# Second tile of q by the casting queue, a new order of the beginning, and whole feed-forward blocks in the first token group

## The chip, the cores and the metric

The kernel runs on one core of a Trainium2 chip. The metric is the device time of one execution in microseconds, as the median of several runs. A profile of one execution gives its span and the work of each engine: PE (matrix products, with PEld for its weight loads), DVE (vector engine), ACT (scalar engine), POOL (GpSimd), and SP, which only issues transfers here.

## The reference

Two steps follow each other. The first is a cosine-weighted linear attention over 8 batches of 8 heads, 576 positions and 64 dimensions. The second is a gated feed-forward block on 4608 tokens of 512 values, with 1536 hidden values.

```
phi(x) = concat(relu(x) * cos(theta), relu(x) * sin(theta))     theta = pi/2 * position / 576
kv  = sum over s of phi(k)[s, f] * v[s, d]        z = sum over s of phi(k)[s, f]
out = (phi(q) @ kv) / (phi(q) @ z + 1e-6)
x   = out, heads side by side: 4608 tokens x 512
g   = x @ w_gate      val = x @ w_val
y   = (silu(g) * val) @ w_out
```

All inputs and the output are float32 in memory. The kernel computes in bfloat16 and accumulates in float32.

## The kernel before, in words

**Tokens.** Each batch has NC = 9 slots of 64 positions. Two slots make a tile of 128 tokens, and four tiles make a group of 512 tokens (GH = 8 slots, T = 512). There are nine groups. The first group is tiles 0 to 3 and needs slots 0 to 7 of batch 0. Its beginning is written by hand; the groups after it follow a plan of slots (`at`, `slot`).

**Loads.** The sync queue (`nc.sync`, SP) carries what must come first, in float32: v of batch 0 in two parts, q slots 0 and 1, k of batch 0 in three parts, then q slots 2 and 3 (`load_first`, L115 to L126). The casting queue (`nc.gpsimd`, POOL) carries the rest and turns float32 into bfloat16 on its way: q slots 4 to 7 of batch 0, the gate and value weights in pieces (`load_w`), k, v and q of batch 1, the output weights (`load_wo`), then batch 2. One small copy on POOL (`hold`, L574) keeps it from issuing before the first part of v is there. `CUT` says where a batch's q is split into two loads.

**The beginning.** A list of words (L619) gives the order in which the instructions of the first group are written. Each engine has its own queue and works through it in that order, waiting where it must. The words, with the tile or part in their digits and the engine after @:

- `cq` casts a slot of q from float32 to bfloat16 (`cast_q`, L337); `tq` turns a tile of q on PE by products with the identity (`turn_q`, L341); `qr` is the relu of the turned q (`relu_turned`); `qw` multiplies it by cosines (part 0) or sines (part 1) on DVE (`weight_q`, L359).
- `rk` is the relu of a part of k, from float32 to bfloat16 (L223); `kv` the products of k and v (`kv_first`, L304); `kvo` the copy of a half of kv from the accumulation banks to memory (`kv_first_out`, L326). `kvo00` and `kvo01` are the two halves for j = 0, `kvo10` and `kvo11` those for j = 1.
- `a` is the attention product of a tile (`a_tile`, L366), `den` and `rec` the denominators and their reciprocals, `x` the normalised tile, `xt` its turning on PE, `xc` the copy of the turned tile to `xT`.
- `G`, `V`, `s`, `m` are one feed-forward block of 128 hidden values: gate products, value products, silu on ACT, multiplication on DVE. `G2.01` is block 2 for tiles 0 and 1, `G1.0` block 1 for tile 0 alone.
- `z` are products with zeros that nobody reads; they keep PE running.

In `turn_q` the tiles 0 and 1 come from `qf`, which `cq` has written, with four full transposes. The tiles 2 and 3 come from the bfloat16 tile `raws[0, "q"]`, in eight transposes of half width.

**The accumulation banks.** There are 8 banks of 512 float32 columns. `take` hands out those used longest ago. A block for 256 tokens fits gate and value into one bank; for 512 tokens it takes two.

**The later blocks of the first group.** Blocks 6 to 11 run in two halves of 256 tokens: blocks f and f+1 for the first half ("a"), then both for the second ("b"). After each, `slot` runs what is planned there: the relu of k of batch 1 (a8, a9), `vmul` for batch 1 (a10, a11, b8, b9), the turning of the last slot of q of batch 0 (b9), and at b11 the turning of q of batch 1 and its kv products. Then come 12 pieces of output products (`steps0`, L707) with tiles 4 to 7 of attention between them (`a_` at slots (0, 0) to (1, 3)). From then on groups run whole blocks of 512 tokens.

Of the kernel before, what the change touches and what calls it, by code (L numbers as in the profile page):

```python
# [10 lines left out]
FP32 = mybir.dt.float32  # L11
# [7 lines left out]
def kernel(  # L19
# [11 lines left out]
    B, H, S, D = q.shape  # L31
    P = 128
    G = H // 2
    J = G // 2
    SH = 64
    NC = S // SH
    d_model, d_ff = moe_w_gate.shape
    KC = d_model // P
    FC = d_ff // P
# [3 lines left out]
    GH = 8  # L43
# [3 lines left out]
    consts = ctx.enter_context(tc.tile_pool(name="consts", bufs=1))  # L47
# [18 lines left out]
    def take(n, hold=None):  # L66

        free = [b for b in range(0, 8, n) if not any(b <= x < b + n for r in held.values() for x in r)]
        b0 = min(free, key=lambda b: sorted(used[b:b + n], reverse=True))
        if hold is not None:  # L70
            held[hold] = range(b0, b0 + n)
        touch(range(b0, b0 + n))
        return banks[:, b0] if n == 1 else banks[:, b0:b0 + n]
# [6 lines left out]
    def give_back(hold):  # L80
        touch(held.pop(hold))
# [4 lines left out]
    def source(b, nm):  # L86
        t = {"q": q, "k": k, "v": v}[nm]
        return t[b].rearrange("(g e) (p c) d -> (e p) g (c d)", e=2, c=NC)

    def raw_of(b, nm):  # L90
        if (b, nm) not in raws:
            raws[b, nm] = raw.tile([P, G, NC, D], BF16, name=f"raw_{nm}")
        return raws[b, nm]

    def load(b, nm, parts=1):
        t, sv, n = raw_of(b, nm), source(b, nm), G // parts
        for i in range(parts):
            sl = slice(i * n, (i + 1) * n)
            nc.gpsimd.dma_start(out=t[:, sl].rearrange("p g c d -> p g (c d)"), in_=sv[:, sl])

    def load_slots(b, nm, lo, hi):
        nc.gpsimd.dma_start(out=raw_of(b, nm)[:, :, lo:hi].rearrange("p g c d -> p g (c d)"),
                            in_=source(b, nm)[:, :, lo * D:hi * D])


    CUT = (4, 7)
    wo_sb = consts.tile([P, FC, d_model], BF16)
    hts = [consts.tile([P, FC, T], BF16, name=f"ht_{i}") for i in range(2)]
    first = {"q": consts.tile([P, G, CUT[0], D], FP32, name="first_q")}

    for nm, home in (("v", wo_sb), ("k", hts[1])):
        flat = home.rearrange("p a b -> p (a b)")[:, 0:2 * G * NC * D]
# [2 lines left out]
    def load_first(nm, gs, lo=0, hi=NC):  # L115
        nc.sync.dma_start(out=first[nm][:, gs, lo:hi].rearrange("p g c d -> p g (c d)"),  # L116
                          in_=source(0, nm)[:, gs, lo * D:hi * D])
# [5 lines left out]
    load_first("k", slice(0, 2))  # L123
    load_first("k", slice(2, 4), 0, KCUT)
    load_first("k", slice(2, 4), KCUT, NC)
    load_first("q", slice(0, G), 2, 4)  # L126
    NW = 8
    pos = consts.tile([P, NC], FP32)
    nc.gpsimd.iota(pos, pattern=[[1, NC]], base=0, channel_multiplier=NC, allow_small_or_imprecise_dtypes=True)
# [6 lines left out]
    for j in range(2):  # L136
        t = consts.tile([P, 8 * J * D1], BF16, name=f"kvd_{j}")
# [50 lines left out]
    for j in range(2):  # L188
        t = consts.tile([P, G, NC, 2, W], BF16, name=f"v2_{j}")
# [10 lines left out]
    def load_w(i, n=2):  # L200

        fs = slice(i * P, (i + n) * P)
        nc.gpsimd.dma_start(out=wg_sb[:, :, fs], in_=wg_r[:, :, fs])
        nc.gpsimd.dma_start(out=wv_sb[:, :, fs], in_=wv_r[:, :, fs])

    def load_wo(i):
        cs = slice(4 * i, 4 * i + 4)
        nc.gpsimd.dma_start(out=wo_sb[:, cs], in_=wo_r[:, cs])
# [10 lines left out]
    def relu_k(b, lo, hi, eng):  # L219
        o = raw_of(b, "k")[:, lo:hi]  # L220
        relu_op(eng, o, o)
# [38 lines left out]
    def qturn_pe(b, j, lo, hi, eng):  # L260
        ps = take(1).bitcast(BF16).rearrange("p (c x) -> p c x", x=P)
        for c in range(lo, hi):
            for i in range(2):
                nc.tensor.transpose(out=ps[i * D:(i + 1) * D, c - lo], in_=raws[b, "q"][:, 2 * j + i, c],  # L264
                                    identity=ident)
        relu_op(eng, qt_of(b)[:, :, j, lo:hi].rearrange("p e c s -> p c e s"),
                ps[:, 0:hi - lo].rearrange("p c (e s) -> p c e s", e=2))
# [33 lines left out]
    def kv_free(b):  # L301
        give_back(("kv", b))
# [38 lines left out]
    def turn_q(t):  # L341
        ps = take(1, ("tq", t)).bitcast(BF16).rearrange("p (y e s) -> p y e s", e=2, s=SH)
        for j in range(J):
            for c in range(2):
                y = 2 * j + c
                if t < 2:
                    nc.tensor.transpose(out=ps[:, y].rearrange("p e s -> p (e s)"),
                                        in_=qf[:, c, j].rearrange("p i d -> p (i d)"), identity=ident)
                    continue
                for i in range(2):  # L350
                    nc.tensor.transpose(out=ps[i * D:(i + 1) * D, y].rearrange("p e s -> p (e s)"),  # L351
                                        in_=raws[0, "q"][:, 2 * j + i, 2 * t + c], identity=ident)
        st["tq", t] = ps[:, 0:2 * J].rearrange("p y e s -> p e y s")
# [136 lines left out]
    def ffn_mm(tg, fc, lo=0, hi=GH, which=(0, 1)):  # L490

        n = (hi - lo) * SH
        ts = slice(lo // 2, hi // 2)
        fs = slice(fc * P, (fc + 1) * P)
        if 0 in which:
            if 2 * n <= 512:
                both = take(1, ("f", tg, fc, lo))
                st["f", tg, fc, lo] = [both[:, 0:n], both[:, n:2 * n]]
            else:
                st["f", tg, fc, lo] = [take(1)[:, 0:n] for _ in range(2)]  # L500
        for i in which:
            for kc in range(KC):
                nc.tensor.matmul(out=st["f", tg, fc, lo][i], lhsT=(wg_sb, wv_sb)[i][:, kc, fs], rhs=xT[tg][:, ts, kc],  # L503
                                 start=(kc == 0), stop=(kc == KC - 1))
# [14 lines left out]
    def ffn_act(*a):  # L519
        ffn_silu(*a)  # L520
        ffn_mul(*a)

    def ffn_fc(*a):

        ffn_mm(*a)
        ffn_act(*a)
# [45 lines left out]
    hold = consts.tile([P, 1], FP32)  # L572
    hold2 = consts.tile([1, 2], BF16)
    nc.gpsimd.tensor_copy(out=hold, in_=first["v"][:, 1, 0, 0:1])  # L574
    load_slots(0, "q", CUT[0], NW)
    load_w(0, 1)
    load_w(1, 1)
    for i in (2, 4, 6):
# [3 lines left out]
    load_slots(0, "q", NW, NC)  # L582
    load_w(10)
    load(1, "v", 2)
    load_slots(1, "q", 0, CUT[1])
    load_wo(0)
    load_wo(1)
    load_wo(2)
    load_slots(1, "q", CUT[1], NC)
    for nm in ("q", "k", "v"):  # L590
        load(2, nm)

# [4 lines left out]
    def at(s, *fns):  # L597
        plan.setdefault(s, []).extend(fns)

    def slot(s):  # L600
        for f in plan.pop(s, ()):
            f()

    def a_(t, j):
        return lambda: (a_half(t, j), x_norm(t) if j else None)
# [2 lines left out]
        return lambda: x_turn(t, fast)  # L608

    def q_(b, j, part, eng="act"):  # L610
        lo, hi = ((0, CUT[b]), (CUT[b], NC))[part]
        return lambda: qturn_pe(b, j, lo, hi, eng)


# [2 lines left out]


    words = """  # L619
        cq0@act cq1@act tq0 qr0@dve rk1.0@act rk0.0@dve qw0.0 qw0.1 z6 kv0.0 rk2.0@act rk3.0@dve rk2.1@act  # L620
        kv1.0 kvo01@dve rk3.1@act cq3@dve kv1.1 cq2@dve kvo00@dve tq1 kvo10@act a0.0 qr1@dve kvo11@act qw1.1
        z2 a0.1 qw1.0 tq2 den0 rec0 a1.0 x0.0 qr2@act tq3 x0.1 xt0.0 a1.1 qw2.0 xc0.0@act xt0.1 qw2.1
        xc0.1@act den1 z2 a2.0 rec1 qr3@act G1.0 x1.0 a2.1 G0.0 s1.0 V0.0 qw3.0 s0.0 xt1.0 qw3.1 V1.0
        xc1.0@dve a3.0 a3.1 m0.0 G1.1 den3 G2.01 m1.0 s1.1 rec3 V1.1 x3.0 s2.01 G0.1 V0.1 s0.1 V2.01 m1.1
        m0.1 xt3.0 den2 m2.01 G3.01 rec2 V3.01 x2.0 s3.01 G4.01 xc3.0@dve G5.01 s4.01 m3.01 xt2.0 s5.01
        V4.01 xc2.0@dve V5.01 m4.01 G2.23 m5.01 G0.23 s2.23 V0.23 s0.23 G3.23 m0.23 V2.23 s3.23 G4.23 m2.23
        V4.23 s4.23 V3.23 m4.23 G1.23 m3.23 V1.23 s1.23 G5.23 m1.23 V5.23 s5.23 m5.23
    """.split()
    halves = (slice(0, KC // 2), slice(KC // 2, KC))
    for word in words:  # L630
        word, _, eng = word.partition("@")
        op, a, b = re.match(r"([A-Za-z]+)(\d+)\.?(\d*)", word).groups()
        whole, a, part = b not in ("0", "1") or a != "0", int(a), int(b or 0)
# [39 lines left out]
                ffn_mul(0, a, *span)  # L673


    order = []
    for f in range(6, FC, 2):
        order += [("a", g) for g in (f, f + 1)]
        order += [("b", g) for g in (f, f + 1)]

    def turn_last():
        for j in range(J):
            qturn_pe(0, j, NC - 1, NC, "act")
# [1 line left out]
    at("b9", turn_last)  # L685
    at("a8", lambda: relu_k(1, 0, 2, "dve"))
    at("a9", lambda: relu_k(1, 2, 4, "dve"))
    for g, s in enumerate(("a10", "a11", "b8", "b9")):
        at(s, lambda g=g: vmul(1, g))
    at("b11", q_(1, 0, 0), q_(1, 1, 0), lambda: kv_mm(1), lambda: kv_out(1))  # L690
    at((0, 0), lambda: kv_free(1), a_(4, 0))
    at((0, 1), a_(4, 1))
    at((0, 2), a_(5, 0))
    at((0, 3), a_(5, 1))
    at((1, 0), turn(4, True), a_(6, 0))
# [3 lines left out]
    at((2, 0), turn(6, True))  # L699
    at((2, 1), q_(1, 0, 1), q_(1, 1, 1))  # L700
    at((2, 2), turn(7, True))
    HALF = GH // 2
    for nm, f in order:
        ffn_fc(0, f, *((HALF, GH) if nm == "b" else (0, HALF)))
        slot(f"{nm}{f}")

    steps0 = [(piece, t) for piece in range(3) for t in range(2)] + [(piece, t) for t in (2, 3) for piece in range(3)]  # L707
    for i, (piece, t) in enumerate(steps0):
# [10 lines left out]
    for b in range(2, B):  # L719
        s0 = SLOTS * (b - 1)  # L720
# [16 lines left out]
    for t in range(2 * OUT, NTG * OUT):  # L737
        tg, i = divmod(t, OUT)
        s = SLOTS * (tg - 1) + (5 if tg > 2 else 4) + 2 * i
# [8 lines left out]
    for tg in range(1, NTG):  # L748
        s0 = SLOTS * tg
# [40 lines left out]
```

## Time and profile before

| What | Value |
|---|---|
| Time, median of 3 runs | 327.97 us (327.35 to 328.61) |
| Span of the profiled execution | 326.1 us (that run took 327.92 us) |
| Granted PE clock | 1.0 |
| First transfer issued by SP | 0.74 us |
| First transfer issued by POOL | 4.50 us |
| First feed-forward product | 18.07 us |
| First block for half of the tokens after the words (block 6) | 30.17 us |
| First output product | 43.16 us |
| First product of group 1 | 57.13 us |

Some landings, as start of issue plus the time to landing that the trace gives:

| Transfer | Queue | Issued | Landed |
|---|---|---|---|
| q slots 0, 1 | sync | 1.75 | 7.6 |
| k, heads of the first half | sync | 2.27 | 9.5 |
| k, second half, slots 0 to 4 | sync | 2.8 | 10.3 |
| k, second half, slots 5 to 8 | sync | 3.3 | 11.4 |
| q slots 2, 3 | sync | 3.84 | 13.65 |
| q slots 4 to 7 | casting | 4.50 | 13.0 |
| gate weights, block 0 | casting | 5.39 | 14.2 |
| value weights, block 1 | casting | 7.59 | 16.5 |
| gate / value weights, blocks 2 and 3 | casting | 8.32 / 9.05 | 17.7 / 19.1 |
| gate weights, blocks 4 and 5 | casting | 9.79 | 20.4 |
| gate / value weights, blocks 8 and 9 | casting | 16.81 / 18.01 | 28.6 / 30.5 |
| q of batch 1, slots 0 to 6 | casting | 27.51 | 38.3 |
| output weights, three parts | casting | 29.11, 31.04, 31.8 | 40.8, 43.3, 45.9 |

How to read the profile's lines. A line in order of time gives start and length in microseconds, engine, line of the code, operation, what it writes and reads, the number of instructions merged, and in brackets how long the engine stood idle before it and what released it. The chain of waits is followed back from the last instruction, at each step to what released it. A queue's line gives its packets, megabytes as written, and the time its packets took as a share of 16 engines.

### The profile page before, as it was taken

How to read it: one execution, taken by the hardware profiler on the slowest of the kernel's cores; microseconds unless marked ns; L12 is line 12 of the kernel's file. 1: busy time of each engine (PE TensorE's matmuls, PEld its weight loads, DVE VectorE, ACT ScalarE, POOL GpSimd, SP SyncE). 2: the span in 40 equal slices, each digit the busy share in tenths (PEclk: the TensorE clock that was granted, in tenths of full speed). 3: DMA queues.
4: the chain of work that ended last, by engine and by line, in shares of the span. 5: the costliest groups of instructions: out<-in, count | busy, mean ns of one | idle time of the engine just before them, and what ended most of it. 6: DMA issues, size and time to landing. Idle time of an engine off the chain costs nothing.

```text
span 326.1 us, 6192 instructions
## 1 busy us (share of the span) xinstructions
PE 318.7 (98%) x2459; PEld 165.0 (51%) x2470; DVE 182.3 (56%) x367; ACT 132.8 (41%) x248; POOL 34.1 (10%) x57
## 2 busy tenths in 40 slices
PE   8799999999999999999999999999999999999995
PEld 4488855454545444544454445444454445444443
DVE  7594857885575655575557555655664145423420
ACT  7353456843463336423543344343432133213311
POOL 6654300002001100020002000200000000000000
PEclk9999999999999999999999999999999999999999
DMA  7999999398867997799598949795921411140014
GB/s 259 224 199 197 207 204 211 62 132 137 162 117 95 163 140 146 110 157 158 121 124 127 181 110 136 108 184 116 138 51 34 99 32 32 36 105 21 2 32 97
DMA packets 71660, 40.51 MB, mean 124 GB/s; under 512 B 46672, under 2 KB 66384, under 8 KB 71632
## 3 DMA queue, kind: packets, MB, share of 16 engines
q1 hardware_dynamic: 49808, 22.55, 39.0%
q0 software_dynamic: 21664, 17.44, 35.2%
q8 instruction: 19, 0.31, 0.4%
q10 hardware_dynamic: 160, 0.13, 0.1%
q14 instruction: 9, 0.07, 0.1%
HBM read 37.75 MB, written 9.44 MB: 145 GB/s over the span
## 4 chain that ended last, share of the span: by engine, by line
PE 94%; DMA 3%; SPq 1%; issue 0%; ACT 0%; DVE 0%; ACTq 0%; DVEq 0%
PE banks L503 57%; PE banks L539 28%; DMA first_q<-in_q_dram 3%; PE banks L276 3%; PE banks L390 2%; SPq L116 1%; PE banks L475 1%; PE banks L434 1%; PE banks L372 1%; PE banks L558 1%; PE banks L264 0%; PE banks L149 0%; ACT ob L561 0%; PE banks L351 0%; DVE qf L339 0%
## 5 line engine op out<-in xcount | busy, mean ns | idle before, releaser
L514 DVE TENSOR_TENSOR ht<-sg,banks 128x512 bf16<-128x512 bf16 (+2 forms) x122 | 76.0, 625 | 67.2 <-PE banks L503 60.9
L509 ACT ACTIVATE sg<-banks 128x512 bf16<-128x512 f32 (+2 forms) x122 | 66.9, 548 | 113.8 <-PE banks L503 108.7
L503 PE MATMUL banks<-xT,wv_sb 128*128 128x512 bf16 (+2 forms) x488 | 112.8, 355 | 0.0
L503 PE MATMUL banks<-xT,wg_sb 128*128 128x512 bf16 (+2 forms) x488 | 112.8, 355 | 0.0
L539 PE MATMUL banks<-wo_sb,ht 128*128 128x512 bf16 x409 | 93.5, 379 | 0.6
L503 PEld LDWEIGHTS <-wv_sb 128*128 128x128 bf16 x488 | 47.1, 98 | 46.4
L503 PEld LDWEIGHTS <-wg_sb 128*128 128x128 bf16 x488 | 45.7, 98 | 41.5
L539 PEld LDWEIGHTS <-ht 128*128 128x128 bf16 x420 | 40.0, 98 | 45.2 <-issue 0.4
L546 ACT COPY ob<-banks 128x512 f32<-128x512 f32 x18 | 10.6, 586 | 51.4 <-PE banks L539 49.4
L232 DVE TENSOR_TENSOR r_q<-raw_q,tab 128x1152 bf16<-128x1152 bf16 x24 | 17.9, 753 | 20.2 <-ACT raw_q L215 20.2
L546 DVE COPY ob<-banks 128x512 f32<-128x512 f32 x17 | 11.7, 691 | 28.9 <-PE banks L539 28.0
L236 DVE TENSOR_TENSOR v<-raw_v,tab 128x1152 bf16<-128x1152 bf16 x31 | 23.0, 751 | 0.3 <-ACT raw_v L570 0.3
L411 DVE TENSOR_TENSOR x<-banks,rec 128x512 bf16<-128x512 f32 (+1 forms) x32 | 21.5, 674 | 1.1
L714 POOL COPY hold<-phit 1x2 bf16<-1x2 bf16 x5 | 0.9, 176 | 156.6 <-DMA phit<-r_q 156.6
L215 ACT ACTIVATE raw_k<-raw_k 128x576 bf16<-128x576 bf16 x24 | 16.0, 675 | 0.0
L215 ACT ACTIVATE raw_q<-raw_q 128x576 bf16<-128x576 bf16 x24 | 15.7, 680 | 0.5 <-DMA raw_q<-in_q_dram 0.5
L390 PEld LDWEIGHTS <-phit 128*128 128x128 bf16 (+1 forms) x240 | 9.9, 100 | 6.0 <-issue 1.3
L390 PE MATMUL banks<-kv,phit 128*128 128x65 bf16 (+1 forms) x240 | 11.5, 195 | 0.0
L149 PE MATMUL banks<-zeros 128*128 128x64 bf16 (+1 forms) x66 | 9.9, 310 | 1.0 <-DVE zeros L144 1.0
L299 DVE CAST kv<-banks 64x260 bf16<-64x260 f32 x12 | 5.1, 428 | 7.5 <-ACT kv L299 7.4
L276 PEld LDWEIGHTS <-raw_k 64*64 64x64 bf16 x504 | 7.5, 106 | 2.6 <-issue 2.1
L276 PE MATMUL banks<-v,raw_k 64*64 64x130 bf16 x504 | 8.7, 218 | 0.0
(80 smaller groups left out, 136.3 us busy)
## 6 DMA issues: line engine op xcount, KB each, us to landing
out_dram<-ob SPq DMA_DIRECT2D x70, 128.0 KB, 2.4
raw_k<-in_k_dram POOLq DMA_DIRECT2D x7, 576.0 KB, 9.7
raw_q<-in_q_dram POOLq DMA_DIRECT2D x6, 576.0 KB, 6.1
raw_v<-in_v_dram POOLq DMA_DIRECT2D x6, 576.0 KB, 12.3
wo_sb<-in_moe_w_out_dram POOLq DMA_DIRECT2D x3, 512.0 KB, 12.3
wg_sb<-in_moe_w_gate_dram POOLq DMA_DIRECT2D x5, 256.0 KB, 10.6
wv_sb<-in_moe_w_val_dram POOLq DMA_DIRECT2D x5, 256.0 KB, 10.0
wo_sb<-in_v_dram SPq DMA_DIRECT2D x2, 576.0 KB, 4.1
```

What stands on the lines that cost most here:

```text
L149: nc.tensor.matmul(out=ps, lhsT=zeros, rhs=zeros[:, 0:cols].unsqueeze(1).to_broadcast([P, 4, cols]), start=True, stop=True)
L215: nc.scalar.activation(out=out, in_=in_, func=AF.Relu)
L232: nc.vector.tensor_tensor(out=st[b, "q"][:, g], in0=o.unsqueeze(2).to_broadcast([P, NC, 2, D]), in1=tab, op=ALU.mult)
L236: nc.vector.tensor_tensor(out=v2s[b % 2][:, g, :, :, 0:D], in0=(first if b == 0 and g == 0 else {"v": raw_of(b, "v")})["v"][:, g].unsqueez ...
L276: nc.tensor.matmul(out=ps[i * D:(i + 1) * D, e, j * 2 * D1:(j + 1) * 2 * D1], lhsT=raws[b, "k"][es, g, c], rhs=v2s[b % 2][es, g, c, :, 0:D ...
L390: nc.tensor.matmul(out=ps[ms, e, g * D1:(g + 1) * D1], lhsT=phit[b][:, e, g, c:c + n].rearrange("p c s -> p (c s)"), rhs=kv2s[b % 2][:, e, ...
L411: nc.vector.tensor_tensor(out=st["x", t].rearrange("p (y e d) -> p e y d", e=2, d=D)[:, :, ys], in0=ps[:, :, 0:2 * J * D1].rearrange("p e ...
L503: nc.tensor.matmul(out=st["f", tg, fc, lo][i], lhsT=(wg_sb, wv_sb)[i][:, kc, fs], rhs=xT[tg][:, ts, kc], start=(kc == 0), stop=(kc == KC - 1))
L509: nc.scalar.activation(out=sg[:, 0:n], in_=st["f", tg, fc, lo][0], func=AF.Silu)
L514: nc.vector.tensor_tensor(out=hts[tg % 2][:, fc, r:r + n], in0=st.pop(("s", tg, fc, lo))[:, 0:n], in1=ps[1], op=ALU.mult)
L539: nc.tensor.matmul(out=o_ps[t], lhsT=hts[tg % 2][:, fc, r:r + P], rhs=wo_sb[:, fc], start=(fc == 0), stop=(fc == FC - 1))
L546: (nc.scalar.copy if t % 2 == 0 else nc.vector.tensor_copy)(out=ob, in_=ps)
```

## The change

The second tile of q (slots 2 and 3) leaves the sync queue. It goes as the first transfer into the casting queue, so it arrives as bfloat16 and needs no cast; its turning then uses the eight half-width transposes that tiles 2 and 3 use. The order of the beginning is written anew for this: copies of kv move to ACT, relus of k to DVE, tile 3 comes before tile 2, and the products of blocks 0, 4 and 5 are placed elsewhere. Blocks 6 to 11 of the first group run for all 512 tokens at once, so what was planned behind the halves gets new places: slot a of block f and slot b of block f now follow each other directly. The vmul of batch 1 moves to b9, a10, b10 and a11; tile 4's two attention halves stand side by side.

```diff
-    CUT = (4, 7)
+    QCUT = 2
+    CUT = 7
...
-    first = {"q": consts.tile([P, G, CUT[0], D], FP32, name="first_q")}
+    first = {"q": consts.tile([P, G, QCUT, D], FP32, name="first_q")}
...
-    load_first("q", slice(0, G), 2, 4)
...
-                if t < 2:
+                if t == 0:
...
-    load_slots(0, "q", CUT[0], NW)
+    load_slots(0, "q", QCUT, 4)
+    load_slots(0, "q", 4, NW)
...
-        cq0@act cq1@act tq0 qr0@dve rk1.0@act rk0.0@dve qw0.0 qw0.1 z6 kv0.0 rk2.0@act rk3.0@dve rk2.1@act
-        kv1.0 kvo01@dve rk3.1@act cq3@dve kv1.1 cq2@dve kvo00@dve tq1 kvo10@act a0.0 qr1@dve kvo11@act qw1.1
-        z2 a0.1 qw1.0 tq2 den0 rec0 a1.0 x0.0 qr2@act tq3 x0.1 xt0.0 a1.1 qw2.0 xc0.0@act xt0.1 qw2.1
-        xc0.1@act den1 z2 a2.0 rec1 qr3@act G1.0 x1.0 a2.1 G0.0 s1.0 V0.0 qw3.0 s0.0 xt1.0 qw3.1 V1.0
-        xc1.0@dve a3.0 a3.1 m0.0 G1.1 den3 G2.01 m1.0 s1.1 rec3 V1.1 x3.0 s2.01 G0.1 V0.1 s0.1 V2.01 m1.1
-        m0.1 xt3.0 den2 m2.01 G3.01 rec2 V3.01 x2.0 s3.01 G4.01 xc3.0@dve G5.01 s4.01 m3.01 xt2.0 s5.01
-        V4.01 xc2.0@dve V5.01 m4.01 G2.23 m5.01 G0.23 s2.23 V0.23 s0.23 G3.23 m0.23 V2.23 s3.23 G4.23 m2.23
-        V4.23 s4.23 V3.23 m4.23 G1.23 m3.23 V1.23 s1.23 G5.23 m1.23 V5.23 s5.23 m5.23
+        cq0@act cq1@act tq0 qr0@dve qw0.0 qw0.1 rk1.0@act rk0.0@dve z8 kv0.0 rk3.0@dve rk2.0@dve kv1.0
+        kvo00@act rk3.1@dve kvo01@act rk2.1@dve kv1.1 tq1 kvo10@act kvo11@dve a0.0 qr1@dve a0.1 qw1.0 tq3
+        qw1.1 tq2 den0 qr3@act rec0 x0.0 a1.0 a1.1 qr2@act x0.1 xt0.0 qw3.1 xt0.1 xc0.0@act qw3.0 xc0.1@act
+        den1 z2 a3.0 rec1 G1.0 x1.0 a3.1 s1.0 G0.0 V0.0 qw2.0 s0.0 xt1.0 qw2.1 V1.0 xc1.0@dve a2.0 a2.1 m1.0
+        G1.1 den3 den2 V1.1 rec3 s1.1 G2.01 x3.0 G3.01 s2.01 m1.1 V2.01 rec2 s3.01 x2.0 xt3.0 V3.01
+        xc3.0@act m2.01 xt2.0 m3.01 G5.01 xc2.0@dve G4.01 s5.01 m0.0 G0.23 s4.01 V0.23 s0.23 G1.23 m0.23
+        G5.23 s1.23 V1.23 s5.23 V4.01 m1.23 V5.23 m4.01 V5.01 m5.23 G2.23 m5.01 V2.23 s2.23 G3.23 m2.23
+        V3.23 s3.23 G4.23 m3.23 V4.23 s4.23 G0.1 m4.23 V0.1 s0.1 m0.1
...
-    for g, s in enumerate(("a10", "a11", "b8", "b9")):
+    for g, s in enumerate(("b9", "a10", "b10", "a11")):
         at(s, lambda g=g: vmul(1, g))
...
-    at((0, 0), lambda: kv_free(1), a_(4, 0))
-    at((0, 1), a_(4, 1))
+    at((0, 0), lambda: kv_free(1), a_(4, 0), a_(4, 1))
...
-    for nm, f in order:
-        ffn_fc(0, f, *((HALF, GH) if nm == "b" else (0, HALF)))
-        slot(f"{nm}{f}")
+    for f in range(6, FC):
+        ffn_fc(0, f)
+        slot(f"a{f}")
+        slot(f"b{f}")
```

More of the change, by code (lines that the diff above doesn't have):

```diff
@@ L584 @@
     load(1, "v", 2)
-    load_slots(1, "q", 0, CUT[1])
+    load_slots(1, "q", 0, CUT)
     load_wo(0)
@@ L588 @@
     load_wo(2)
-    load_slots(1, "q", CUT[1], NC)
+    load_slots(1, "q", CUT, NC)
     for nm in ("q", "k", "v"):
@@ L610, in q_ @@
     def q_(b, j, part, eng="act"):
-        lo, hi = ((0, CUT[b]), (CUT[b], NC))[part]
+        lo, hi = ((0, CUT), (CUT, NC))[part]
         return lambda: qturn_pe(b, j, lo, hi, eng)
     words = """
-        cq0@act cq1@act tq0 qr0@dve rk1.0@act rk0.0@dve qw0.0 qw0.1 z6 kv0.0 rk2.0@act rk3.0@dve rk2.1@act
-        kv1.0 kvo01@dve rk3.1@act cq3@dve kv1.1 cq2@dve kvo00@dve tq1 kvo10@act a0.0 qr1@dve kvo11@act qw1.1
-        z2 a0.1 qw1.0 tq2 den0 rec0 a1.0 x0.0 qr2@act tq3 x0.1 xt0.0 a1.1 qw2.0 xc0.0@act xt0.1 qw2.1
-        xc0.1@act den1 z2 a2.0 rec1 qr3@act G1.0 x1.0 a2.1 G0.0 s1.0 V0.0 qw3.0 s0.0 xt1.0 qw3.1 V1.0
-        xc1.0@dve a3.0 a3.1 m0.0 G1.1 den3 G2.01 m1.0 s1.1 rec3 V1.1 x3.0 s2.01 G0.1 V0.1 s0.1 V2.01 m1.1
-        m0.1 xt3.0 den2 m2.01 G3.01 rec2 V3.01 x2.0 s3.01 G4.01 xc3.0@dve G5.01 s4.01 m3.01 xt2.0 s5.01
-        V4.01 xc2.0@dve V5.01 m4.01 G2.23 m5.01 G0.23 s2.23 V0.23 s0.23 G3.23 m0.23 V2.23 s3.23 G4.23 m2.23
-        V4.23 s4.23 V3.23 m4.23 G1.23 m3.23 V1.23 s1.23 G5.23 m1.23 V5.23 s5.23 m5.23
+        cq0@act cq1@act tq0 qr0@dve qw0.0 qw0.1 rk1.0@act rk0.0@dve z8 kv0.0 rk3.0@dve rk2.0@dve kv1.0
[6 more added lines that the diff above has]
+        V3.23 s3.23 G4.23 m3.23 V4.23 s4.23 G0.1 m4.23 V0.1 s0.1 m0.1
     """.split()
@@ L673 @@
                 ffn_mul(0, a, *span)
[L676 to L679, printed above, removed]
     def turn_last():
@@ L701 @@
     at((2, 2), turn(7, True))
-    HALF = GH // 2
-    for nm, f in order:
-        ffn_fc(0, f, *((HALF, GH) if nm == "b" else (0, HALF)))
-        slot(f"{nm}{f}")
+    for f in range(6, FC):
+        ffn_fc(0, f)
+        slot(f"a{f}")
+        slot(f"b{f}")
     steps0 = [(piece, t) for piece in range(3) for t in range(2)] + [(piece, t) for t in (2, 3) for piece in range(3)]
```

## The prediction

> **What bounds the kernel now.** I read the page first (engines, chain), then the chain in order of time, then DVE, PE and ACT in order of time for the first 50 us, then each queue's traffic in one-microsecond stretches, and last the groups by shape.
>
> The page, its parts 1 and 4:
>
> ```profile
> PE 318.7 (98%) x2459; PEld 165.0 (51%) x2470; DVE 182.3 (56%) x367; ACT 132.8 (41%) x248; POOL 34.1 (10%) x57
> PE 94%; DMA 3%; SPq 1%; issue 0%; ACT 0%; DVE 0%; ACTq 0%; DVEq 0%
> ```
>
> PE carries the chain except for a stretch at the beginning. So two things can help: fewer PE nanoseconds, or an earlier start of dense products. The chain in order of time names what holds that start (start, length):
>
> ```profile
> 3.84 9.83 DMA first_q<-in_q_dram
> 13.76 0.60 DVE qf L339 x2
> ```
>
> This is the transfer of q slots 2 and 3 (the second tile), last in the sync queue, landing 9.8 us after issue, and then its two casts. DVE in order of time shows what stands behind it:
>
> ```profile
> 10.96 0.43 DVE L324 CAST kvd<-banks 128x260 bf16<-128x260 f32 x1
> 13.76 0.58 DVE L339 CAST qf<-first_q 128x256 bf16<-128x256 f32 x2 [2.37 <-DMA first_q<-in_q_dram]
> 14.27 0.41 DVE L324 CAST kvd<-banks 128x260 bf16<-128x260 f32 x1
> 14.84 0.42 DVE L217 TENSOR_SCALAR qr<-banks 128x512 bf16<-128x512 bf16 x1 [0.15 <-PE banks L347]
> 15.30 0.76 DVE L360 TENSOR_TENSOR qwT<-qr,tabq 128x512 bf16<-128x512 bf16 x2
> 16.41 0.76 DVE L411 TENSOR_TENSOR x<-banks,rec 128x256 bf16<-128x256 f32 x2
> ```
>
> DVE stands still for 2.37 us. The kvd cast at 14.27 (word kvo00) needs nothing of q, yet stands behind the q casts in DVE's queue, and the first attention product a0.0 needs that kvd. From 13.76 on DVE hardly pauses. PE in order of time over the same stretch:
>
> ```profile
> 11.96 0.73 PE L316 MATMUL banks<-v,raw_k 64*64 64x130 bf16 x16 [0.31 <-ACT raw_k L215]
> 14.40 0.40 PE L347 MATMUL banks<-ident,qf 128*128 128x128 bf16 x4 [1.71 <-DVE qf L339]
> 18.07 0.39 PE L503 MATMUL banks<-xT,wg_sb 128*128 128x128 bf16 x4
> 43.16 1.04 PE L539 MATMUL banks<-wo_sb,ht 128*128 128x512 bf16 x3
> ```
>
> The first feed-forward product (G1.0) is at 18.07. From there to 57.13, where group 1 begins, summing the products at their steady pace gives about 38.8 us for 39.06 us of time. So what G1.0 gains is gained at the end, if its successors find their data.
>
> **What the Trainium skill says.** DMA: Bandwidth & Descriptors, section Queues, rings and completion order: each engine goes round robin between its queues, packet by packet. The trace agrees. Traffic of the casting queue (q0) and the sync queue (q1) in 8 to 9, 9 to 10 and 10 to 11 us (packets, MB, share):
>
> ```profile
> q1 hardware_dynamic: 293, 0.36, 101.8%
> q0 software_dynamic: 6, 0.00, 2.3%
> ...
> q1 hardware_dynamic: 243, 0.21, 71.0%
> q0 software_dynamic: 141, 0.07, 52.0%
> ...
> q0 software_dynamic: 200, 0.10, 73.8%
> q1 hardware_dynamic: 203, 0.12, 54.2%
> ```
>
> Once both move, packets are nearly equal. But the casting queue, which issued at 4.50, moves nothing before about 8.9. The same page, section SWDGE vs HWDGE vs iDMA: casting during a transfer belongs to the GpSimd-issued queue. The trace agrees: q from sync passes L339, raw_q does not. TensorE: Matmul & The Clock Gate, section Back-to-back issue gap: N/2.4 ns plus 2.5 ns. The trace agrees: four 256-column products every 0.437 us (109 ns each), four of 512 every 0.864 us (216 ns).
>
> **The change part by part.**
>
> 1. *q slots 2 and 3.* Sync loses its last transfer (256 KB); the casting queue gets it ahead of slots 4 to 7. The two DVE casts (0.58 us) go. The tile has 512 rows of 512 bytes, so 512 packets. From 8.9 they run beside some 240 packets left of k; at the 384 to 403 packets/us of the two mixed windows, and up to 700/us once alone (q0 moved 703 packets in 13 to 14 us, of the same 256-byte written size), they are through at about 10.5 to 10.8. Slots 4 to 7 were through at about 11.9 by the same count and landed at 13.0, so I add 1.1: landing 11.6 to 11.9, I take 11.7, against 13.65. The bytes read in total are the same, so slots 4 to 7 and the weights behind should land as before (13.0, then 14.2 on). One more transfer in a queue that lets eight be outstanding delays only issues whose ring is already backed up.
>
> 2. *tq1 by raw_q*: eight half-width transposes in place of four. Groups of eight (L351) went from 15.72 to their reader at 16.18 (0.46), groups of four from 14.40 to 14.84 (0.44). Cost 0.02 to 0.05, beside DVE's kvo11.
>
> 3. *The new order up to qr1.* k's last piece lands at 11.4. DVE then does rk3.1 and rk2.1: 256 elements each, priced from 320 at 0.31 (L217 at 10.72) as 0.27; bounds 0.25 and 0.36 (ACT's price). That gives 11.47 to 12.0. The 16 products of kv1.1 took about 0.44 from their last input: 12.06 to 12.5. kvo11 on DVE 12.53 to 12.95, with kvo10 beside it on ACT; tq1 on PE 12.35 to 12.8, q having landed 0.6 before. qr1 so starts at about 12.92 instead of 14.84: 1.92 earlier. ACT takes kvo00 and kvo01 near 11.3, where it is idle, so neither waits for q.
>
> 4. *qr1 to G1.0.* The DVE order is the same in kind: qr1, two weightings, den, rec, x0 in halves, two weightings, den, rec, x1. That was 3.23 us from 14.84 to 18.07. Now 12.92 + 3.23 = 16.15. What could be later: qr3 and qr2 on ACT (0.60 each, from about 14.2) end at 15.4, about when xc0.0 is wanted (15.35); tq3 stands ahead on PE and needs slots 4 to 7 at 13.0. Both fit. One z2 (0.43 us) fewer on PE was idle filling.
>
> 5. *G1.0 to the last first-group block.* Same products, other order; fc 4 and 5's V go late. Needs against landings before: V2.01 at 19.35 (19.1), G5.01 at 20.65 (20.4), block 8 at about 31.7 (gate 28.6, value 30.5), block 10 at about 35.2 (33.2), q of batch 1 at 39.0 (38.3). All hold, by 0.25 to 3 us. Blocks 6 to 11 whole: each had 4 x 0.437 = 1.748, now 2 x 0.864 = 1.728; 6 x 0.02 = 0.12 us less. DVE's shape rows: 2 x 0.419 becomes 0.686 a block, ACT's 2 x 0.384 becomes 0.597; neither is the bound.
>
> 6. *vmul moved* to b9, a10, b10, a11, the last now behind the whole-block multiply of fc 11. DVE from the end of block 9: multiply 0.62, relu 0.36, vmul 0.67 (starts to starts); in block 10, 0.62 + 2 x 0.67; so block 11's multiply starts 0.33 late and the last vmul ends about 1.6 after block 11. kv_mm(1)'s second half is due 28 transposes (0.97) and 36 products (0.59) after it: 1.56. A stall of 0.1 (0 to 0.3).
>
> 7. *Output side.* First products with wo_sb at 43.16 - 1.9 = 41.25, against landings at 40.8, 43.3 and 45.9 for the three pieces; their uses would be 41.25, 43.9 and 46.1. It holds by 0.2 to 0.6. a4.0 and a4.1 side by side change the order, not the work.
>
> Sum: 1.92 + 0.12 - 0.03 (late transposes) - 0.12 (stall) = 1.89 us. 327.97 - 1.9 = 326.1.
>
> **The rivals.**
>
> *A wall of transfers (rival A).* Everything from 19 us to 46 us now has 0.2 to 0.6 of slack, where it had 2. If the casting queue's whole train lands 0.9 later (more small packets, or k and q in each other's way), wo_sb's third piece lands at 46.8 in place of 45.9 and its use moves from 46.1 to 46.8: a gain of 1.9 - 0.7 = 1.2, 326.8. q slots 2 and 3 at 13.0, as the first transfer of that queue landed before, gives much the same: tq1 13.1, qr1 13.55, gain 1.3, 326.7. For it: nothing moved in this queue for 4.4 us after issue. Against: equal bytes, equal packets.
>
> *Slower (rival B).* q and the weights land 3 us late, because 512 further small packets put off everything in one serial queue: 327.97 + (3 - 2.1) = 328.9, since the first wo_sb uses had 2.1 us of slack. Or the whole blocks make PE wait for banks and for DVE: in blocks 9 to 11 DVE has 1.65, 1.96 and 1.29 us against PE's 1.73. Against it: the excess is 0.33, and four blocks fit into the banks.
>
> *Better (rival C).* k lands 0.3 sooner without q beside it, and the early stalls vanish: gain 2.7, 325.3.
>
> **How the numbers follow.** My forecast 0.58, A 0.27, B 0.08, C 0.07. The forecast's time is 326.1. The bound of 0.5% is 1.64 us, at 326.33: the forecast case lies 0.23 below it, so about four fifths of that case are beyond it, with C and a little of A: faster 0.56. Within 0.5%: the rest of the case, and most of A: 0.36. Slower 0.08. The range 325.3 to 327.9 takes in C's value at one end, A with all its delays at the other, and leaves out B.
>
> **What would show it.** Right: no first_q in the chain after the first tile; tq1 (now L351) near 12.4; qr1 near 12.9; G1.0 at 16.0 to 16.3; slots 4 to 7 still landing at 13.0; group 1 starting near 55.2; no wait above 0.3 at 39 to 47 us. Wrong: raw_q as what tq1 waited for past 12.6; wg_sb, wv_sb or wo_sb as the releaser of PE between 18 and 47 us; kv_mm(1) waiting long for DVE; or G1.0 early and group 1 not.

## The result, and the profile after

| | Before | After |
|---|---|---|
| Time, median | 328.29 us (4 runs, 327.35 to 328.61) | 326.10 us (4 runs, 325.89 to 326.49) |
| Ratio, with its 95% interval | | 0.9939 (0.9915 to 0.9964) |
| Second measurement, later | 327.80 us (12 runs) | 326.45 us (7 runs), ratio 0.9941 (0.992 to 0.9963) |
| Span of the profiled execution | 326.1 us | 324.7 us |
| tq1, second tile of q turned | 14.40 | 12.56 |
| qr1 | 14.84 | 13.06 |
| G1.0, first feed-forward product | 18.07 | 16.34 |
| Block 6 | 30.17 | 28.68 |
| 28 transposes before kv_mm(1) | 41.08 | 39.47 |
| First output product | 43.16 | 41.91 |
| First product of group 1 | 57.13 | 55.62 |

The kernel is faster, by about 0.6%; both intervals lie below 1. The medians differ by 1.35 to 2.2 us, the two profiles by 1.4 to 1.5. One part of this difference is a second gain that these two profiles do not show; it has its own experiment below.

The chain in order of time of the kernel after (start, length, what):

```profile
1.75 6.00 DMA first_q<-in_q_dram
7.77 0.72 ACT qf L339 x2
9.38 0.76 DVE qwT L360 x2
10.14 0.75 DVE raw_k L217
10.93 0.72 PE banks L316 x30
13.50 0.76 DVE qwT L360 x2
...
38.61 0.99 DVE v L236 x2
41.26 0.71 PE banks L276 x34
```

The only `first_q` in it is that of the first tile. The 9.83 us of transfer for the second are gone. The chain now runs from the first tile of q through its weightings on DVE (9.38) and the relu of k that stands behind them (10.14) to the kv products on PE (10.93). A new link stands at 38.61: DVE's `vmul` of batch 1, for which PE waits in `kv_mm(1)`.

DVE after, in order of time:

```profile
10.05 1.69 DVE L217 TENSOR_SCALAR raw_k<-ht 128x576 bf16<-128x576 f32 x5
12.71 0.43 DVE L324 CAST kvd<-banks 128x260 bf16<-128x260 f32 x1 [0.97 <-PE banks L316]
13.06 0.41 DVE L217 TENSOR_SCALAR qr<-banks 128x512 bf16<-128x512 bf16 x1
13.50 0.76 DVE L360 TENSOR_TENSOR qwT<-qr,tabq 128x512 bf16<-128x512 bf16 x2
```

The idle 2.37 us before the q casts became 0.97 us before the copy of kv, and `qr1` needs no wait of its own any more. PE after, in order of time:

```profile
12.56 0.41 PE L351 MATMUL banks<-ident,raw_q 128*64 128x128 bf16 x8
...
16.34 0.38 PE L503 MATMUL banks<-xT,wg_sb 128*128 128x128 bf16 x4
...
40.37 1.61 PE L276 MATMUL banks<-v,raw_k 64*64 64x130 bf16 x72
41.91 1.04 PE L539 MATMUL banks<-wo_sb,ht 128*128 128x512 bf16 x4
42.88 0.64 PE L434 MATMUL banks<-kvd,phit 128*64 128x260 bf16 x8
...
45.18 0.38 PE L434 MATMUL banks<-kvd,phit 128*128 128x260 bf16 x2
```

From these starts the 1.51 us up to group 1 can be told apart:

| Stretch | Before | After | Difference |
|---|---|---|---|
| to G1.0 | 18.07 | 16.34 | -1.73 |
| G1.0 to block 6 | 12.10 | 12.34 | +0.24 |
| block 6 to the 28 transposes | 10.91 | 10.79 | -0.12 |
| transposes and kv_mm(1) | 2.08 | 2.44 | +0.36 |
| output pieces to group 1 | 13.97 | 13.71 | -0.26 |

### The profile page after: what moved, and what is told of

It reads as the page before. It is cut to its first block, busy times and chain, and to the rows that moved or that the text cites. A ratio compares the mean times of both kernels' runs of the same rounds, so it can differ in the third digit from the quotient of the medians.

```text
span 324.7 us, 6106 instructions
## 1 busy us (share of the span) xinstructions
PE 319.0 (98%) x2426; PEld 160.2 (49%) x2426; DVE 181.2 (56%) x360; ACT 131.6 (41%) x241; POOL 34.9 (11%) x58
## 4 chain that ended last, share of the span: by engine, by line
PE 93%; DVE 2%; DMA 2%; ACT 0%; issue 0%; SPq 0%; ACTq 0%; DVEq 0%
PE banks L503 57%; PE banks L539 28%; PE banks L390 2%; PE banks L276 2%; DMA first_q<-in_q_dram 2%; PE banks L475 1%; PE banks L434 1%; DVE v L236 1%; PE banks L558 1%; DVE qwT L360 0%; PE banks L316 0%; DVE ht L514 0%; PE banks L372 0%; SPq L117 0%; DVE qr L217 0%
## 5 line engine op out<-in xcount | busy, mean ns | idle before, releaser
L514 DVE TENSOR_TENSOR ht<-sg,banks 128x512 bf16<-128x512 bf16 (+2 forms) x116 | 74.9, 650 | 69.5 <-PE banks L503 66.1
L509 ACT ACTIVATE sg<-banks 128x512 bf16<-128x512 f32 (+2 forms) x116 | 65.8, 568 | 113.3 <-PE banks L503 108.9
L503 PE MATMUL banks<-xT,wg_sb 128*128 128x512 bf16 (+2 forms) x464 | 111.6, 364 | 0.0
L503 PEld LDWEIGHTS <-wv_sb 128*128 128x128 bf16 x464 | 44.8, 98 | 49.0 <-issue 0.4
L503 PEld LDWEIGHTS <-wg_sb 128*128 128x128 bf16 x464 | 43.3, 98 | 43.5
L390 PE MATMUL banks<-kv,phit 128*128 128x65 bf16 (+1 forms) x240 | 11.5, 195 | 0.0
```

Source lines behind the costliest of these rows:

```text
L390: nc.tensor.matmul(out=ps[ms, e, g * D1:(g + 1) * D1], lhsT=phit[b][:, e, g, c:c + n].rearrange("p c s -> p (c s)"), rhs=kv2s[b % 2][:, e, ...
L509: nc.scalar.activation(out=sg[:, 0:n], in_=st["f", tg, fc, lo][0], func=AF.Silu)
L514: nc.vector.tensor_tensor(out=hts[tg % 2][:, fc, r:r + n], in0=st.pop(("s", tg, fc, lo))[:, 0:n], in1=ps[1], op=ALU.mult)
```

## The experiments

The theory: the gain comes before G1.0, from the transfer of q's second tile; the whole blocks give 0.12 us and lose more to `vmul`. The rivals: the new order of words makes the gain; the whole blocks carry a part of it; or the casts could have been got out of the way without moving the transfer.

**1. The beginning alone** (`front_only`): the changed kernel with the second half of before.

```diff
-    for f in range(6, FC):
-        ffn_fc(0, f)
-        slot(f"a{f}")
-        slot(f"b{f}")
+    for nm, f in order:
+        ffn_fc(0, f, *((HALF, GH) if nm == "b" else (0, HALF)))
+        slot(f"{nm}{f}")
...
-    for g, s in enumerate(("b9", "a10", "b10", "a11")):
+    for g, s in enumerate(("a10", "a11", "b8", "b9")):
```

> The new loads and the new order of the beginning, with blocks 6 to 11 in halves and the vmul of batch 1 where they were before. Theory (the gain is made before the first feed-forward product, the second half of the change is worth about nothing or less): G1.0 near 16.3 as in the changed kernel, kv_mm(1) without a wait inside its 72 products (1.25 us long, not 1.61), block halves 0.12 us longer in sum; group 1 begins at 55.62 - 0.36 + 0.12 = 55.4, time 0.1 to 0.3 us below the changed kernel, near 325.9. Rival (the whole blocks carry a good part of the gain): group 1 at 56.2 or later, time 326.7 or more.

Measured: 326.3 us (8 runs), ratio 0.9947 (0.9928 to 0.9967). G1.0 at 15.80 in its profile, `kv_mm(1)` 1.35 us long, group 1 at 55.25. The beginning alone has the whole gain. Its G1.0 is 0.54 us earlier than that of the changed kernel, with the same beginning: the first q had landed earlier (casts at 7.40, not 7.77). So single profiles of one beginning differ by half a microsecond at G1.0; smaller differences need a stretch within a profile, or the times of many runs.

**2. The second half alone** (`back_only`): the kernel before with the whole blocks and the moved `vmul`.

```diff
+    for f in range(6, FC):
+        ffn_fc(0, f)
+        slot(f"a{f}")
+        slot(f"b{f}")
...
+    for g, s in enumerate(("b9", "a10", "b10", "a11")):
```

> The beginning of before, with the whole blocks and the moved vmul of the change. Theory: G1.0 stays at 18.07; whole blocks give back 0.12, the last vmul makes kv_mm(1) wait 0.3 to 0.4; group 1 at 57.2 to 57.5, time 0.1 to 0.3 above before: no change that times can tell. Rival (whole blocks carry a good part): group 1 at 56.6 or earlier.

Measured: 328.56 us (20 runs), ratio 1.001 (0.9997 to 1.0023): no gain. `kv_mm(1)` took 1.60 us, as expected. Group 1 came at 58.01, later than the 57.2 to 57.5 that were expected, since G1.0 stood at 19.10 instead of 18.07, although nothing before it was changed. The stretches of one microsecond from 13 to 18 us of this run show why (engine busy times, then the granted PE clock, then transfers):

```profile
core 0: us, PE busy (x) PEld busy (x) DVE busy (x) ACT busy (x) POOL busy (x), PEclk, DMA share, GB/s
...
13.00:14.00 1.00, 0.00 (x0) 0.00 (x0) 0.54 (x2) 0.09 (x1) 0.74 (x1) 1.00 1.81 178
14.00:15.00 1.00, 0.80 (x10) 0.63 (x11) 0.85 (x3) 0.00 (x0) 0.93 (x2) 1.00 1.71 189
15.00:16.00 1.00, 1.00 (x10) 0.57 (x10) 0.83 (x4) 0.00 (x0) 1.00 (x2) 0.53 1.56 190
16.00:17.00 1.00, 1.00 (x14) 0.63 (x14) 0.93 (x4) 0.44 (x1) 0.60 (x2) 0.50 1.46 197
17.00:18.00 1.00, 1.00 (x14) 0.83 (x14) 0.94 (x3) 0.16 (x2) 0.60 (x2) 0.50 1.45 196
```

PE stands idle for 1.79 us up to 14.20, waiting for the q casts. From about 15 to 18.5 us it is granted half its clock. The profile of before had the same idle stretch and a full clock. Over its runs the mean granted clock falls in two groups: of the 29 runs of before beside this experiment, 17 had 0.998 or 1.0 and a median of 327.64 us, 12 had 0.992 to 0.995 and 328.89 us. Of the 20 runs of this experiment 12 were in the lower group. The 8 others have a median of 327.71 us, so the whole blocks show no gain with the full clock either. The changed kernel had 0.997 or more in all of its 11 runs.

**3. The transfer alone** (`transfer_only`): q's second tile by the casting queue, the old words less cq2 and cq3, the old second half.

```diff
-        kv1.0 kvo01@dve rk3.1@act cq3@dve kv1.1 cq2@dve kvo00@dve tq1 kvo10@act a0.0 qr1@dve kvo11@act qw1.1
+        kv1.0 kvo01@dve rk3.1@act kv1.1 kvo00@dve tq1 kvo10@act a0.0 qr1@dve kvo11@act qw1.1
```

> q slots 2 and 3 by the casting queue, with the old order of words less cq2 and cq3, and the old second half. Theory (both count: the transfer frees kvo00 and tq1, the order saves DVE and PE places besides): tq1 near 12.8, qr1 near 13.3, G1.0 near 16.7, group 1 near 55.8, time 1.2 to 1.5 below before. Rival A (the transfer alone is the whole gain): G1.0 at 16.3 or earlier. Rival B (the order is the gain, the transfer does little): G1.0 at 17.5 or later.

Measured: 326.02 us (5 runs), ratio 0.9933 (0.991 to 0.9956). tq1 at 12.15, qr1 at 12.61, G1.0 at 15.84, group 1 at 55.26. My theory, which gave the order a share, fell; rival A is right: the transfer alone has the gain, and the new order adds nothing that can be seen (run 1, with the new order and the old second half on the same chip, took 326.11 to 326.63 us, this run 325.85 to 326.23). With the old words DVE waits at the same place, for the turned tile:

```profile
10.71 0.76 DVE L324 CAST kvd<-banks 128x260 bf16<-128x260 f32 x2
12.61 0.42 DVE L217 TENSOR_SCALAR qr<-banks 128x512 bf16<-128x512 bf16 x1 [1.14 <-PE banks L351]
```

With the casts gone, kvo00 follows kvo01 at once in the old order too. The move changes two things together: q lands earlier, and its casts fall away. No run separates them. In the changed kernel q lies ready for 1.06 us (landed at 11.5, tq1 at 12.56), longer than the two casts took (0.58), so by this estimate the landing is the larger part. An earlier place for this tile within the sync queue was not tried.

**4. vmul one step earlier** (`vmul_early`): the changed kernel with the relu of k at a7, so that `vmul` can run at b8.

```diff
-    at("a8", lambda: relu_k(1, 0, 2, "dve"))
-    at("a9", lambda: relu_k(1, 2, 4, "dve"))
-    for g, s in enumerate(("b9", "a10", "b10", "a11")):
+    at("a7", lambda: relu_k(1, 0, 2, "dve"), lambda: relu_k(1, 2, 4, "dve"))
+    for g, s in enumerate(("b8", "b9", "a10", "b10")):
```

> The changed kernel with the relu of k of batch 1 at slot a7 and its vmul at b8, b9, a10, b10, one step earlier, so that no vmul stands behind the multiply of block 11. Theory (kv_mm(1) waits 0.36 us for the last vmul on DVE): its 72 products take 1.25 us again, group 1 begins 0.3 to 0.4 us earlier, at 55.25, span 324.35. Rival (something else, banks or the weights, fills the place): group 1 within 0.1 of 55.62. If v of batch 1 lands too late for b8, the multiply of block 9 on DVE waits for it, and PE would show it at the banks.

Measured: 326.02 us (5 runs). PE of this run, in order of time:

```profile
40.22 1.25 PE L276 MATMUL banks<-v,raw_k 64*64 64x130 bf16 x72
```

The wait is gone, 1.61 became 1.25. From G1.0 (16.19) to group 1 (55.13) this run takes 38.94 us, the changed kernel 39.28: 0.34 less, so what the wait took is kept to the end of the group. The times of whole runs are too close to show it (326.10 and 326.45 for the changed kernel).

**5. The idle stretch filled** (`before_fill`): the kernel before, with six products of zeros where PE stood idle.

```diff
-        kv1.0 kvo01@dve rk3.1@act cq3@dve kv1.1 cq2@dve kvo00@dve tq1 kvo10@act a0.0 qr1@dve kvo11@act qw1.1
+        kv1.0 kvo01@dve rk3.1@act cq3@dve kv1.1 cq2@dve kvo00@dve z6 tq1 kvo10@act a0.0 qr1@dve kvo11@act qw1.1
```

> The kernel before with six products of zeros (1.3 us) written ahead of tq1, in the place where PE stands idle for 1.7 us; nothing else. In 12 of the 29 runs of the kernel before taken so far the mean granted clock was 0.992 to 0.995, and these took 328.9 us against 327.6 for the other 17; the profile of the run with the old beginning and whole blocks shows the clock at one half from 15 to 18.5 us, right after that idle stretch. Theory (the idle stretch lets the clock fall): no run below 0.997, median 327.6, G1.0 still near 18.1. Rival (the fall of the clock has another cause, or filling does not count): two groups of runs as before, median near 328.

Measured: 327.63 us (21 runs), ratio 0.9978 (0.9968 to 0.9988). None of its 21 runs had a clock below 0.997; of the 51 runs of before taken beside it, 27 had (medians 327.73 and 328.86). Its G1.0 was at 17.53 in the one profile, with the first q and k landing earlier there (qr0 at 8.23); the median is that of the full-clock runs of before. So work that nobody reads, put into the gap, is worth 0.2% on the mean: the lower clock cost 1.1 to 1.3 us in about half of the runs. The kernels with q in the casting queue get this too: none of their 42 runs was below 0.997. That a shorter gap is the reason is not shown, for run 6 kept its clock with a gap of 1.88 us.

**6. q back in the sync queue** (`sync_naive`): the changed kernel, order and whole blocks kept, only q's second tile as before.

```diff
-    QCUT = 2
+    QCUT = 4
...
+    load_first("q", slice(0, G), 2, 4)
...
-        kvo00@act rk3.1@dve kvo01@act rk2.1@dve kv1.1 tq1 kvo10@act kvo11@dve a0.0 qr1@dve a0.1 qw1.0 tq3
+        kvo00@act rk3.1@dve kvo01@act rk2.1@dve kv1.1 kvo10@act kvo11@dve cq3@act cq2@dve tq1 a0.0 qr1@dve a0.1 qw1.0 tq3
```

> The changed kernel with q slots 2 and 3 back in the sync queue and two casts (cq3 on ACT, cq2 on DVE, both behind the copies of kv), the rest of the new order and the whole blocks kept. Theory (the transfer is the gain): q lands near 13.6, tq1 near 14.2, qr1 near 14.6, G1.0 near 17.9, time 327.6 to 328.6, no gain that counts. Rival (the order, with kvo00 no longer behind the casts, is the gain): G1.0 below 17.0.

Measured: 328.03 us (12 runs), ratio 0.9992 (0.9979 to 1.0005). tq1 at 14.34, qr1 at 14.77, G1.0 at 18.07. Without the transfer there is no gain, although no copy of kv stands behind a cast here. All 12 runs had the full clock; beside the runs of before that had it too (327.73 us), this kernel is 0.3 us slower; from G1.0 to group 1 it takes 39.35 us, before 39.06.

**7. Tile 0 first** (`order_only`): q still by sync, but the words carry tile 0 to its end ahead of tq1.

```diff
-        kvo00@act rk3.1@dve kvo01@act rk2.1@dve kv1.1 tq1 kvo10@act kvo11@dve a0.0 qr1@dve a0.1 qw1.0 tq3
+        kvo00@act rk3.1@dve kvo01@act rk2.1@dve kv1.1 kvo10@act kvo11@dve a0.0 a0.1 cq3@act cq2@act den0 rec0
+        x0.0 x0.1 xt0.0 tq1 tq3 xt0.1 xc0.0@act xc0.1@act qr1@dve qw1.0 qw1.1 tq2 a1.0 a1.1 qr3@act den1 rec1
...
```

> q slots 2 and 3 in the sync queue with casts on ACT, but tile 0 is carried to its end first: a0.0, a0.1, den0, rec0, x0 stand ahead of tq1 and qr1, so that only tile 1 waits for q. Whole blocks kept. Theory (what costs is that tile 0 stands behind q in the queues, so an order without the new transfer can have most of the gain): G1.0 near 15.7, bound by the gate weights that land at 15.6; xt1.0 near 17.2 as in the changed kernel; group 1 within 0.3 of 55.62; time near 326.3. Rival (q has to come earlier, whatever the order): G1.0 may be early, but PE stands idle after it until xt1.0 at 18 or later, group 1 at 56.6 or later, time above 327.

Measured: 328.32 us (20 runs), ratio 1.0006 (0.9995 to 1.0016). G1.0 was early, at 16.18, but PE then ran dry, as this excerpt in order of time shows:

```profile
16.18 0.61 PE L504 MATMUL banks<-xT,wg_sb 128*128 128x128 bf16 x8
16.62 0.39 PE L504 MATMUL banks<-xT,wv_sb 128*128 128x128 bf16 x4
17.56 0.40 PE L476 MATMUL banks<-ident,x 128*128 128x128 bf16 x4 [0.56 <-DVE x L412]
```

G1.1 came at 19.51 where the changed kernel has it at 18.21, and group 1 at 56.99. The rival is right: an early first product is worth nothing if the second tile is not there.

**8. The best of the parts** (`both_best`): the transfer with the old words, whole blocks, and `vmul` early.

```diff
-        kvo00@act rk3.1@dve kvo01@act rk2.1@dve kv1.1 tq1 kvo10@act kvo11@dve a0.0 qr1@dve a0.1 qw1.0 tq3
+        kv1.0 kvo01@dve rk3.1@act kv1.1 kvo00@dve tq1 kvo10@act a0.0 qr1@dve kvo11@act qw1.1
...
-    for g, s in enumerate(("b9", "a10", "b10", "a11")):
+    for g, s in enumerate(("b8", "b9", "a10", "b10")):
```

> The transfer of the change with the old order of words (less cq2 and cq3), the whole blocks, and the relu and vmul of batch 1 one step earlier. Theory (gains add: G1.0 near 16.0 and no wait in kv_mm(1), 0.12 for whole blocks): group 1 at 55.1, time 325.9, 0.2 below the changed kernel. Rival (another wait takes it up): group 1 at 55.5 or later.

Measured: 325.80 us (6 runs, 325.54 to 327.19), ratio 0.9942 (0.9926 to 0.9959). G1.0 at 15.52, group 1 at 54.83. Its PE shows the next bound:

```profile
45.70 1.02 PE L539 MATMUL banks<-wo_sb,ht 128*128 128x512 bf16 x4 [0.43 <-DMA wo_sb<-in_moe_w_out_dram]
```

The third part of the output weights is now what PE waits for.

**9. Both once more on one chip** (`after_again`, `best_again`).

> The changed kernel once more, timed on the same chip as the next one. 326.1 as before; granted clock never below 0.997; against the kernel before a ratio of 0.993 to 0.995.

> The transfer with the old words, whole blocks and early vmul once more, on the same chip as the changed kernel. If the gains of G1.0 and of kv_mm(1) hold, 0.2 to 0.4 below the changed kernel, 325.8; bounded by the last part of wo_sb, for which PE waited 0.43 us in its first profile. If that was one lucky run, the two agree within 0.1.

Measured: the changed kernel 326.45 us (7 runs), ratio to before 0.9941 (0.992 to 0.9963); the other 325.73 us (6 runs), ratio 0.9925 (0.99 to 0.995). Every one of the latter's runs lay between 325.60 and 326.11. The two intervals overlap; its gain over the changed kernel, 0.7 us here and 0.3 against the first measurement, is of the expected sign, and its profile again shows `kv_mm(1)` in 1.24 us and a wait of 0.21 us for `wo_sb`.

**10. The casting queue let go earlier** (`no_hold`):

```diff
-    nc.gpsimd.tensor_copy(out=hold, in_=first["v"][:, 1, 0, 0:1])
```

> The changed kernel without the small POOL copy that keeps the casting queue from issuing before v has landed, so the first casting transfer is issued near 2.6 instead of 4.50. Question: why does this queue move nothing before 8.9 us? If it takes a fixed time from issue (4.4 us), its first packets move near 7.0, q slots 2 and 3 land near 10, and k lands later for it, so that qr1 is not earlier. If it waits until the sync queue's backlog has come down to what the engines hold already, its first packets still move near 8.9 or little before.

Measured: one run, 326.9 us. First issue at 2.46; the packets of both queues in 6 to 7 and 7 to 8 us:

```profile
q1 hardware_dynamic: 252, 0.35, 100.7%
q0 software_dynamic: 1, 0.00, 0.2%
...
q1 hardware_dynamic: 145, 0.29, 87.3%
q0 software_dynamic: 105, 0.03, 26.9%
```

The first packets move about 4.4 us after issue, as in the kernel before (4.50 to about 8.9). So the delay goes with the issue, not with the sync queue's backlog. q's second tile itself landed 8.8 us after its issue, at 11.3, hardly before the 11.5 of the changed kernel; near 10 had been expected. k's last piece came later: its relus on DVE start at 12.04, after a wait for the transfer, where run 4 has them at 11.46, and qr1 is at 13.47. In this one run, letting the queue go earlier does not help.

## Why the prediction was right

The predicted time, 326.1, is the first measured median. Step by step:

*Steps 1 and 2, the transfer.* I put the landing at 11.7. The trace gives 7.0 us from the issue at 4.50, so 11.5. POOL after, in order of time, has the ninth transfer of the casting queue wait for the first:

```profile
11.80 0.74 POOL L203 DMA_DIRECT2D wg_sb<-in_moe_w_gate_dram  x1 [1.21 <-DMA raw_q<-in_q_dram]
```

tq1 came at 12.56, directly behind kv1.1, so q was not what it waited for. The equal share of packets that I had built on was only rough: in 9 to 10 us 302 packets of the casting queue ran beside 203 of the sync queue. The Trainium skill's DMA: Bandwidth & Descriptors (Queues, rings and completion order) lets the queues take turns by packets of several descriptors, while the packets that the profile counts are here about 256 bytes each (717 for 0.18 MB in 13 to 14 us), so that such counts test it only loosely.

*Step 3, up to qr1.* Predicted 12.92, measured 13.06, but not by the path that was summed. The sum let k's last piece, landing at 11.4, decide. In the profile after, DVE goes through its five relus of k from 10.05 to 11.74 without waiting for a transfer, and the chain comes from the first q instead, which landed 0.23 us later than in the profile of before (casts at 7.77 instead of 7.54). What follows it is partly the new order's doing: it puts the weightings of tile 0 ahead of k's relus on DVE, and eight products of zeros in place of six ahead of kv0.0 on PE. In runs 1 and 4, with the same beginning, the chain runs through these eight products, for 1.73 us. Products that nobody reads thus stand on the path; fewer of them were not tried. So the closeness of this step is in part luck. It also named the order as part of the gain; runs 3, 6 and 7 show that it is not needed. The freed kvo00 was the transfer's doing, because the casts that stood before it went.

*Step 4.* 3.23 us from qr1 to G1.0 predicted, 3.28 measured.

*Step 5.* The landings held. The whole blocks gave 0.12 us, as worked out. What I had not seen is 0.24 us between G1.0 and block 6. The new order of words costs it: runs 4, 6 and 10 have 12.33 or 12.34 us there too, run 8, with the old words, 12.10 as before. PE pauses twice for about 0.2 us, up to 19.73 at V2.01 and up to 23.87 at V1.23, each time about 0.05 after the silu of the same block can have ended on ACT (that of block 2 runs from 19.30); in the new words the silu stands ahead of these value products, whose bank it reads, with a single group of other products to cover it. This cause is argued from the times, not tested. The Trainium skill's TensorE: Matmul & The Clock Gate (Back-to-back issue gap), from which the prediction took its formula, gives it for a single product, and for a stream about 131 ns per product of 512 columns; the trace has 216 ns in its streams (0.864 us for four), and the measurement decides.

*Step 6, vmul.* The mechanism was right and the size was off: 0.1 forecast (0.12 in the sum), 0.36 measured, beyond my bound of 0 to 0.3. The last `vmul` ended 1.74 us after block 11 (1.6 forecast), its use was due after 1.49 (1.56 forecast: the transposes were put at their length, 0.97, where the next product starts after 0.90), and the first waiting product started 0.05 later. Run 4 confirms it.

*Step 7.* "a4.0 and a4.1 side by side change the order, not the work" was wrong by 0.25 us, in the change's favour. These products have weights of 64 columns (128*64 in the lines), the output products around them of 128. In before, each of the two halves stood alone between output products:

```profile
44.13 0.44 PE L434 MATMUL banks<-kvd,phit 128*64 128x260 bf16 x4
...
45.47 0.41 PE L434 MATMUL banks<-kvd,phit 128*64 128x260 bf16 x4
...
46.68 0.39 PE L434 MATMUL banks<-kvd,phit 128*128 128x260 bf16 x2
```

Three output pieces with both halves took from 43.16 to 46.68, 3.52 us; after, from 41.91 to 45.18, 3.27 us. The other profiles agree: 3.49 to 3.53 in runs 1, 3 and 5, where the halves stand alone, and 3.27 to 3.30 in runs 2, 4, 6, 7, 8 and 10, where they stand side by side (3.40 in the second profile of run 8's kernel). No run moved the halves and nothing else. The output weights arrived in time for the changed kernel.

*The sum.* 1.89 forecast, 1.4 to 1.5 in the two profiles. The rest of the medians' difference is what the prediction missed altogether: the granted clock. It argued from one profile with a clock of 1.0, while in almost half of the runs of before (44 of 92) the mean granted clock was below 0.997, and these took 1.1 to 1.3 us longer. The errors nearly cancelled: a start 0.2 us later than forecast and 0.5 us of waits beyond those forecast on one side, 0.25 us and the clock on the other. So the exact hit is partly luck.

*The rivals.* A, the wall of transfers, did not bind the changed kernel, but it stands where it was put: with 0.7 to 0.8 us more gained by group 1, PE waits 0.2 to 0.4 us for `wo_sb`. B did not come.

## What to carry to other kernels

When the end of a chain is a transfer with its casts, moving that one transfer to the queue that casts may be the whole gain: test it alone before a new order of instructions is written round it. Here the new order gave nothing before G1.0 and cost 0.24 us after it. Before an engine's work is moved to later slots, add up its queue up to the next use: here 0.36 us were lost to a vector operation that had idle room one block earlier. And look at the granted clock of every run, not of one profile: one profile with the full clock hid a loss of 1.1 to 1.3 us that almost half of the runs had.

## What the runs showed of the hardware

- In the profile of run 2 the granted clock fell to half for about 3.5 us, starting less than 1 us after an idle stretch of PE of 1.79 us. Its mean was below 0.997 in 12 of 20 runs of that kernel and, for before, with the same stretch, in 12 of 29, 27 of 51 and 5 of 12; with six products of zeros in the stretch, in none of 21. The Trainium skill's TensorE: Matmul & The Clock Gate (Why this matters for your kernels) warns of gaps above some 3 us; here a shorter one was enough. It is not the length alone: run 6 had a gap of 1.88 us and no run of 12 below 0.997, run 7, whose longest gap there was 0.96 us, 3 of 20. The eight products of zeros ahead of the first kv products, in place of six, are the nearest difference of run 6, but what exactly decides was not tried.
- Attention products with weights of 64 columns between output products with 128 took about 0.25 us less side by side than apart (3.27 against 3.52 us for the same work; each placement in at least four profiles).
- The first transfer of the casting queue moved its first packet about 4.4 us after its issue, at both times of issue tried. The Trainium skill's DMA: Bandwidth & Descriptors (Latency and other measured facts) has about 1 us for this path's first byte; here the measurement decides, and its cause stays open.
